# Output copies ahead of products, value products behind L1, and a last tile in two column halves

## The chip, the cores and the metric

The kernel runs on one core of a Trainium2 chip. The metric is the device time of one execution in microseconds (us). The kernel before takes 312.5 us (median; 312.0 to 312.8 over the first four runs). One run differs from the next by some tenths of a microsecond, so the questions of this case, which are about 0.1 to 1.2 us, are answered mostly from traces, stage by stage, and only in the sum from times.

Engines are called PE (matmul), DVE (vector), ACT (scalar, activation functions), POOL and SP (which here only starts transfers). PSUM is the memory that matmuls write to; this kernel keeps eight buffers of 512 float32 per partition in it, called banks below.

## The reference

```python
q_bucket, k_bucket = hash bits of q @ proj, k @ proj      # 6 bits each
scores = where(q_bucket == k_bucket, q @ k.T / 8, -1e9)   # 4 batches, 8 heads, 768 tokens, 64 wide
x = softmax(scores) @ v                                   # heads side by side: 3072 x 512
h = x @ w_in                                              # 512 -> 2048   ("L1")
g = h * cos(h)
out = g @ w_out                                           # 2048 -> 512   ("L2")
```

(abridged: the softmax and the reshape are written out in the original.) The output is 3072 x 512 in float32.

## The kernel before

All instructions are emitted in one fixed order, and each engine works through its own in that order. Attention runs head by head in 192 steps: a step makes scores on PE, exponentials on ACT, and value products on PE. L1 of a batch stands in one block inside the attention of the next. L2 of a batch is cut into single matmuls and filled into the gaps by `fill(n)`.

```python
def l1_ff(b, ff, hp):                 # one of 16 L1 tiles of a batch
    ...                               # 8 matmuls of 384 columns into the bank(s) hp
    for c_, g_, h_ in pieces:
        nc.scalar.activation(out=c_, in_=h_, func=ACTF.Sin, bias=cos_bias, scale=1.0)
    for c_, g_, h_ in pieces:
        nc.vector.tensor_tensor(out=g_, in0=h_, in1=c_, op=ALU.mult)   # the product
...
def l2_mm():                          # one L2 matmul; 16 make an output tile
    b, qt, ff = l2q.pop(0)
    if ff == 0 and not state["hold"]:
        state["m"] = 1 - state["m"]   # the other bank, except inside an L1 block
    ...
    if ff == NFF - 1:
        if b == B - 1 and qt == T - 1:            # last tile of all: two half copies
            nc.vector.tensor_copy(out=ob[:, 0:hw], in_=o_ps[:, 0:hw])
            nc.sync.dma_start(out=dst[:, 0:hw], in_=ob[:, 0:hw])
            nc.vector.tensor_copy(out=ob[:, hw:], in_=o_ps[:, hw:])
            nc.scalar.dma_start(out=dst[:, hw:], in_=ob[:, hw:])
        else:
            nc.vector.tensor_copy(out=ob, in_=o_ps)   # the output copy
            nc.sync.dma_start(out=dst, in_=ob)
...
state["hold"] = bb > 0                # the L1 block of batch bb
for ff in range(NFF):
    ...                               # choose the bank hp
    l1_ff(bb, ff, hp)
    ...
    if ff in (0, 1) and len(pend) > 0:
        av_step()                     # six value matmuls
    if bb > 0:
        fill(L1F(ff))                 # 3, 3, 2, 2, then 0, 1, 0, 1 ...
state["hold"] = False
l2_add(bb)
fill(ENDF)
```

The softmax here doesn't subtract the row's maximum and nothing guards it: scores larger than these inputs give would overflow.

Of the kernel before, what the change touches and what calls it, by code (L numbers as in the profile page):

```python
# [9 lines left out]
FP32 = mybir.dt.float32  # L10
# [3 lines left out]
ALU = mybir.AluOpType  # L14
# [8 lines left out]
def kernel(  # L23
# [10 lines left out]
    nc = tc.nc  # L34
    B, H, S, D = q.shape
    assert (B, H, S, D) == (4, 8, 768, 64)
    NBITS = proj.shape[1]
    D_MODEL = H * D
    D_FF = moe_w_out.shape[0]
    P = 128  # L40
    T = S // P
    NP = B * H // 2
    NFT = D_MODEL // P
    NFF = D_FF // P
# [6 lines left out]
    L1F = lambda ff: (3,3,2,2)[ff] if ff<4 else ff%2  # L51
    UF = lambda u: 2 if u % 2==0 else 1
    NEARLY = 5

    glob = ctx.enter_context(tc.tile_pool(name="glob", bufs=1))
    natp = ctx.enter_context(tc.tile_pool(name="nat", bufs=3))
# [10 lines left out]
    obp = ctx.enter_context(tc.tile_pool(name="ob", bufs=3))  # L67
# [3 lines left out]
    wout_t = [glob.tile([P, D_MODEL], FP16, name=f"wout{i}") for i in range(NFF)]  # L71
# [17 lines left out]
    s_ps = [psp.tile([P, 2, 512], FP32, name=f"s_ps{i}") for i in range(2)]  # L89
    av_ps = [psp.tile([P, 512], FP32, name=f"av_ps{i}") for i in range(2)]  # L90
    m_ps = [psp.tile([P, 512], FP32, name=f"m_ps{i}") for i in range(2)]
    state = {"m": 0, "rot": 0, "hold": False}

    nat, blk, bits = {}, {}, {}
    xn, xT = {}, {}
# [5 lines left out]
    def load(pr, eng):  # L101
        nat[pr] = []
        for src, nm in ((q, "natq"), (k, "natk"), (v, "natv")):
            t_ = natp.tile([P, 2, T * D], FP32, name=nm)
            eng.dma_start(out=t_, in_=heads_ap(src, pr))
            nat[pr].append(t_)
# [7 lines left out]
    def n16_rows(pr):  # L114
        return n16x_bufs[pr % 2].rearrange("p h w t e -> p (h w t e)")[:, 0:2 * T * 2 * D].rearrange(
            "p (h t w d) -> p h t w d", h=2, t=T, w=2)

    def cast_qk(pr, hh, engs):
        for w in range(2):
            if pr >= NEARLY:  # L120
                o_ = n16_rows(pr).rearrange("p h t w d -> p (h t) w d")[:, :, w, :]
# [10 lines left out]
    def cast_v(pr):  # L132
        vx = vx_bufs[pr % 3]
        nv = nat[pr][2].rearrange("p h (t d) -> p h t d", d=D)
        nc.gpsimd.tensor_copy(out=vx[:, :, :, 0:D], in_=nv)  # L135
        half = vsp.tile([P, 2, 3, D], FP32, name="vhalf")
        nc.gpsimd.tensor_tensor(out=half, in0=nv[:, :, 0:3, :], in1=nv[:, :, 3:6, :], op=ALU.add)  # L137
        two = vsp.tile([P, 2, D], FP32, name="vtwo")
        nc.gpsimd.tensor_tensor(out=two, in0=half[:, :, 0, :], in1=half[:, :, 1, :], op=ALU.add)
        nc.gpsimd.tensor_tensor(  # L140
            out=vs_bufs[pr % 3][:, :, 0:D], in0=two, in1=half[:, :, 2, :], op=ALU.add)
# [102 lines left out]
    def score(h, jt):  # L244
        pr, hh = divmod(h, 2)
        sp = s_ps[state["rot"] % 2]
        state["rot"] += 1
        for c, (c0, c1) in enumerate(((0, 512), (512, 768))):
            nc.tensor.matmul(  # L249
                out=sp[:, c, 0:c1 - c0],  # L250
                lhsT=kx(pr)[:, hh, jt * P:(jt + 1) * P],
                rhs=qx(pr)[:, hh, c0:c1],
                start=True, stop=True)
        pt = ptp.tile([P, S], FP16, name="pt")
        nc.scalar.activation(  # L255
            out=pt, in_=sp.rearrange("p c n -> p (c n)")[:, 0:S], func=ACTF.Exp,
            bias=exp_bias, scale=EXP_SCALE)
        pts[(h, jt)] = pt
# [52 lines left out]
    g_tiles = {}  # L311

    def l1_ff(b, ff, hp):
        halves = hp if isinstance(hp, list) else [hp[:, c, :] for c in range(2)]
        for ft in range(NFT):
            for c in range(2):
                nc.tensor.matmul(  # L317
                    out=halves[c][:, 0:C2],
                    lhsT=win_t[ft][:, ff * P:(ff + 1) * P],
                    rhs=xT[(b, ft)][:, 3 * c:3 * c + 3, :],  # L320
                    start=(ft == 0), stop=(ft == NFT - 1))
        cos = cosp.tile([P, 2, C2], FP16, name="cos")
        g = gp.tile([P, 2, C2], FP16, name="g")
        if isinstance(hp, list):
            pieces = [(cos[:, c], g[:, c], halves[c][:, 0:C2]) for c in range(2)]
        else:
            pieces = [(cos, g, hp[:, :, 0:C2])]
        for c_, g_, h_ in pieces:
            nc.scalar.activation(out=c_, in_=h_, func=ACTF.Sin, bias=cos_bias, scale=1.0)  # L329
        for c_, g_, h_ in pieces:  # L330
            nc.vector.tensor_tensor(out=g_, in0=h_, in1=c_, op=ALU.mult)  # L331
        g_tiles[(b, ff)] = g

    l2q = []

    def l2_add(b):
        l2q.extend((b, qt, ff) for qt in range(T) for ff in range(NFF))

    def l2_mm():
        b, qt, ff = l2q.pop(0)  # L340
        if ff == 0 and not state["hold"]:
            state["m"] = 1 - state["m"]
        o_ps = m_ps[state["m"]]
        g = g_tiles[(b, ff)].rearrange("p c n -> p (c n)")
        nc.tensor.matmul(  # L345
            out=o_ps, lhsT=g[:, qt * P:(qt + 1) * P], rhs=wout_t[ff],
            start=(ff == 0), stop=(ff == NFF - 1))
        if ff == NFF - 1:
            ob = obp.tile([P, D_MODEL], FP32, name="ob")
            dst = out.rearrange("(b p t) n -> b t p n", b=B, t=T)[b, qt]  # L350
            if b == B - 1 and qt == T - 1:
                hw = D_MODEL // 2
                nc.vector.tensor_copy(out=ob[:, 0:hw], in_=o_ps[:, 0:hw])
                nc.sync.dma_start(out=dst[:, 0:hw], in_=ob[:, 0:hw])
                nc.vector.tensor_copy(out=ob[:, hw:], in_=o_ps[:, hw:])
                nc.scalar.dma_start(out=dst[:, hw:], in_=ob[:, hw:])
            else:
                nc.vector.tensor_copy(out=ob, in_=o_ps)  # L358
                nc.sync.dma_start(out=dst, in_=ob)

    def fill(n):
        for i in range(n):
            if l2q and not (state["hold"] and i > 0 and l2q[0][2] == 0):
                l2_mm()

    def weights_in(i):
# [2 lines left out]
    def weights_out(i):  # L369
        nc.gpsimd.dma_start(out=wout_t[i], in_=moe_w_out[i * P:(i + 1) * P, :])  # L370

    pend = []
# [15 lines left out]
    with tc.manual_schedule():  # L388
# [29 lines left out]
        for b_ in range(4):  # L418
            nc.vector.tensor_copy(
                out=projblk[32 * b_:32 * b_ + 32, :, b_, 0:NBITS], in_=proj2)  # L420
# [30 lines left out]
        def at(u, f):  # L451
            acts.setdefault(u, []).append(f)
# [5 lines left out]
        for n in range(1, NP):  # L458
            s0 = 12 * (n - 1) - (0 if n < NEARLY else 4 if n == NEARLY else 6)
            def start(n=n):  # L460
                cast_qk(n, None, (nc.gpsimd, nc.gpsimd))
                blocks(n)
                cast_v(n)
            if n < NEARLY:
                at(s0 + 2, lambda n=n: load(n + 2, nc.sync if n + 2 < NEARLY else nc.gpsimd))
            elif NEARLY + 1 < n < NP - 1:
                at(s0 - 1, lambda n=n: load(n + 1, nc.gpsimd))
            if n < NEARLY:
                o_ = 3 if n == 1 else 0
# [34 lines left out]
        for u in range(U):  # L504
            h, jt = divmod(u, T)
            score(h, jt)
            pend.append((h, jt))
            for _ in range(2):
                if len(pend) > (4 if u < T else 2):
                    av_step()  # L510
            for f in acts.get(u, ()):
                f()
            b = u // UB
            if b > 0:
                fill(UF(u))
            if u in L1_AT:
                bb = L1_AT[u]
                state["hold"] = bb > 0
                for ff in range(NFF):
                    if bb == 0 and ff % 3 == 2:  # L520
                        hp = m_ps
                    elif ff % 3 == 2:
                        hp = [m_ps[1 - state["m"]], av_ps[0]]
                    else:
                        hp = s_ps[state["rot"] % 2]
                        state["rot"] += 1
                    l1_ff(bb, ff, hp)
                    if bb == 0:
                        nc.gpsimd.tensor_copy(out=mark, in_=g_tiles[(0, ff)][:, 0, 0:1])
                        if ff < NFF // 2:  # L530
                            weights_out(2 * ff)
                            weights_out(2 * ff + 1)
                        elif ff == NFF // 2:
                            load(NEARLY + 2, nc.gpsimd)
                    if ff in (0, 1) and len(pend) > 0:
                        av_step()
                    if bb > 0:
                        fill(L1F(ff))
                state["hold"] = False
                l2_add(bb)  # L540
                fill(ENDF)
# [4 lines left out]
        fill(1000)  # L546
        for ff in range(NFF):
            hp = (s_ps[0], m_ps, s_ps[1])[ff % 3]
            l1_ff(B - 1, ff, hp)
        l2_add(B - 1)  # L550
        fill(1000)

# [29 lines left out]
```

## Time and profile before

| before | value | how to read it |
|---|---|---|
| time | 312.5 us | the profiled run spans 310.8; the rest lies outside the span |
| PE busy | 97% of the span | matmul ends are modelled, so this is no measure of waits |
| PE waits on an output copy | 1.8 us, 2 times | the two at the starts of L1 of batches 1 and 2 |
| PE wait on a product | 0.3 us, once | the end of L1 of batch 0 |

**A ruler.** The trace shows a table load of 1.28 us on ACT each time that it changes between exponential and cosine. These loads stand at the borders of the stages, and their starts cut the run into pieces. Four of them in the timeline of ACT of the kernel before (start us, us, engine, line, operation):

```profile
126.19 1.28 ACT L329 ACT_TABLE_LOAD   x1
151.93 1.28 ACT L255 ACT_TABLE_LOAD   x1
196.50 1.28 ACT L329 ACT_TABLE_LOAD   x1
221.94 1.28 ACT L255 ACT_TABLE_LOAD   x1
```

L1 of batch 1 lasts from 126.19 to 151.93, 25.74 us; the attention after it 44.57; L1 of batch 2 25.44. The piece from the last table load (257.98) to the end of the span is called the last piece below: 310.8 - 257.98 = 52.82 us. Span ends are given to 0.1 us in the views, so a last piece is good to 0.05. Where that is too coarse, "by the records" below means times taken from the single instructions and landings in the packed trace, which are good to 0.01.

### The profile page before, as it was taken

The page shows a single profiled execution, that of the slowest core. Times are in us where ns is not written, and L with a number is a line of the kernel's source. Part 1 is how long each engine was busy: PE and PEld are TensorE (multiplying, and loading weights), DVE is VectorE, ACT ScalarE, POOL GpSimd, SP SyncE. Part 2 cuts the span into 40 slices and gives each one's busy share as a digit, 9 for nine tenths or more (in the row PEclk, how much of TensorE's full clock was granted, in tenths as well). Part 3 has the DMA queues.
Part 4 walks back from the last instruction along what each step waited for, and adds up shares of the span by engine and source line. Part 5 has one row for each costly group of instructions (what it writes and reads, how often), then busy time and mean ns, then how long its engine had stood idle before and what let it go on. Part 6 is the DMA issues. An engine that isn't in the chain of part 4 may idle for free.

```text
span 310.8 us, 7680 instructions
## 1 busy us (share of the span) xinstructions
PE 300.5 (97%) x3074; PEld 181.2 (58%) x3074; DVE 201.5 (65%) x434; ACT 234.1 (75%) x288; POOL 109.1 (35%) x180
## 2 busy tenths in 40 slices
PE   8899999899999999899999999999999999999995
PEld 3577667566566666555566666555566664565442
DVE  3665467877698988756677869757677343477211
ACT  3788999977899999666899999756899993477000
POOL 3897268288484584300064584100030000000000
PEclk9999999999999999999999999999999999999999
DMA  7959959399559976600168988100133222100121
GB/s 213 373 105 187 327 55 216 44 142 179 190 154 253 209 192 152 203 2 0 38 83 235 229 152 194 30 34 0 38 75 90 68 61 86 43 0 0 58 79 69
DMA packets 45332, 37.74 MB, mean 121 GB/s; under 512 B 32264, under 2 KB 39200, under 8 KB 45296
## 3 DMA queue, kind: packets, MB, share of 16 engines
q1 hardware_dynamic: 38080, 19.35, 28.5%
q0 software_dynamic: 6576, 17.17, 21.0%
q10 hardware_dynamic: 640, 0.72, 0.8%
q8 instruction: 24, 0.39, 0.5%
q14 instruction: 12, 0.10, 0.1%
HBM read 27.26 MB, written 6.29 MB: 108 GB/s over the span
## 4 chain that ended last, share of the span: by engine, by line
PE 84%; ACT 9%; DVE 3%; issue 2%; DVEq 0%; ACTq 0%
PE m_ps L345 25%; PE s_ps L317 17%; PE s_ps L249 17%; PE av_ps L275 9%; ACT pt L255 8%; PE m_ps L317 6%; PE m_ps L161 4%; PE av_ps L317 2%; PE s_ps L384 1%; PE m_ps L221 1%; ACT cos L329 1%; DVE ob L358 1%; DVE g L331 1%; DVE blkq L148 1%; PE av_ps L161 1%
## 5 line engine op out<-in xcount | busy, mean ns | idle before, releaser
L255 ACT ACTIVATE pt<-s_ps,exp_bias 128x768 f16<-128x768 f32 x192 | 161.6, 899 | 11.1 <-PE s_ps L249 9.7
L345 PE MATMUL m_ps<-wout,g 128*128 128x512 f16 x384 | 109.1, 379 | 2.1 <-DVE ob L358 1.8
L249 PE MATMUL s_ps<-qx,kx 128*128 128x512 f16 (+1 forms) x384 | 93.8, 326 | 2.6 <-ACT pt L255 1.2
L275 PEld LDWEIGHTS <-pt 128*128 128x128 f16 x1152 | 58.7, 97 | 21.7
L317 PEld LDWEIGHTS <-win 128*128 128x128 f16 x512 | 49.9, 98 | 34.4 <-issue 0.2
L275 PE MATMUL av_ps<-vx,pt 128*128 128x65 f16 x1152 | 65.7, 193 | 0.0
L317 PE MATMUL s_ps<-xT,win 128*128 128x384 f16 x352 | 62.3, 326 | 0.1
L331 DVE TENSOR_TENSOR g<-s_ps,cos 128x768 f16<-128x768 f32 x44 | 42.1, 957 | 29.9 <-ACT cos L329 29.9
L329 ACT ACTIVATE cos<-s_ps,cos_bias 128x768 f16<-128x768 f32 x44 | 39.6, 901 | 27.7 <-PE s_ps L317 26.4
L249 PEld LDWEIGHTS <-kx 128*128 128x128 f16 x384 | 35.2, 97 | 31.1 <-issue 3.3
L345 PEld LDWEIGHTS <-g 128*128 128x128 f16 x384 | 32.8, 98 | 24.4 <-issue 5.7
L135 POOL CAST vx<-natv 128x768 f16<-128x768 f32 x16 | 13.2, 827 | 95.2 <-PE av_ps L275 90.2
L358 DVE COPY ob<-m_ps 128x512 f32<-128x512 f32 x23 | 15.8, 685 | 22.0 <-PE m_ps L345 21.9
L317 PE MATMUL m_ps<-xT,win 128*128 128x384 f16 x120 | 27.6, 326 | 0.0
L329 ACT ACTIVATE cos<-m_ps,cos_bias 128x384 f16<-128x384 f32 x30 | 16.3, 578 | 8.4 <-PE m_ps L317 8.4
L302 DVE TENSOR_TENSOR xn<-tot,rc 128x384 f16<-128x384 f32 x24 | 20.1, 838 | 0.8
L331 DVE TENSOR_TENSOR g<-m_ps,cos 128x384 f16<-128x384 f32 x30 | 15.7, 550 | 2.1 <-ACT cos L329 1.8
L297 DVE COPY dv<-av_ps 128x65 f32<-128x65 f32 x24 | 5.1, 211 | 16.9 <-PE av_ps L275 16.9
L137 POOL TENSOR_TENSOR vhalf<-natv 128x384 f32<-128x384 f32 x16 | 15.9, 995 | 0.0
L130 POOL CAST n16x<-natk 128x768 f16<-128x768 f32 (+1 forms) x16 | 13.0, 810 | 5.8 <-DMA natk<-in_k_dram 5.8
L148 DVE STREAM_TRANSPOSE blkq<-natq 128x768 f32<-128x768 f32 x15 | 14.6, 975 | 0.3
L130 POOL CAST n16x<-natq 128x768 f16<-128x768 f32 (+1 forms) x16 | 13.1, 820 | 4.8 <-DMA natq<-in_q_dram 4.8
(76 smaller groups left out, 267.6 us busy)
## 6 DMA issues: line engine op xcount, KB each, us to landing
out_dram<-ob SPq DMA_DIRECT2D x23, 256.0 KB
natq<-in_q_dram POOLq DMA_DIRECT2D x11, 384.0 KB, 4.1
natk<-in_k_dram POOLq DMA_DIRECT2D x11, 384.0 KB, 4.7
natv<-in_v_dram POOLq DMA_DIRECT2D x11, 384.0 KB, 5.7
win<-in_moe_w_in_dram POOLq DMA_DIRECT2D x4, 512.0 KB, 7.3
wout<-in_moe_w_out_dram POOLq DMA_DIRECT2D x16, 128.0 KB, 4.8
natq<-in_q_dram SPq DMA_DIRECT2D x4, 384.0 KB
natk<-in_k_dram SPq DMA_DIRECT2D x4, 384.0 KB
```

Source lines behind the costliest of these rows:

```text
L130: engs[w].tensor_copy(out=o_, in_=i_)
L137: nc.gpsimd.tensor_tensor(out=half, in0=nv[:, :, 0:3, :], in1=nv[:, :, 3:6, :], op=ALU.add)
L148: nc.vector.transpose(out=blk[pr][w].rearrange("p h t c r -> p (h t c r)"), in_=nat[pr][w].rearrange("p h f -> p (h f)"))
L249: nc.tensor.matmul(out=sp[:, c, 0:c1 - c0], lhsT=kx(pr)[:, hh, jt * P:(jt + 1) * P], rhs=qx(pr)[:, hh, c0:c1], start=True, stop=True)
L255: nc.scalar.activation(out=pt, in_=sp.rearrange("p c n -> p (c n)")[:, 0:S], func=ACTF.Exp, bias=exp_bias, scale=EXP_SCALE)
L275: nc.tensor.matmul(out=bank[:, qt * W:qt * W + D + 1], lhsT=pt[:, qt * P:(qt + 1) * P], rhs=vx_bufs[pr % 3][:, hh, jt, 0:D + 1], start=Fal ...
L302: nc.vector.tensor_tensor(out=dst, in0=tot[:, :, 0:D], in1=rc.unsqueeze(2).to_broadcast([P, T, D]), op=ALU.mult)
L317: nc.tensor.matmul(out=halves[c][:, 0:C2], lhsT=win_t[ft][:, ff * P:(ff + 1) * P], rhs=xT[(b, ft)][:, 3 * c:3 * c + 3, :], start=(ft == 0) ...
L329: nc.scalar.activation(out=c_, in_=h_, func=ACTF.Sin, bias=cos_bias, scale=1.0)
L331: nc.vector.tensor_tensor(out=g_, in0=h_, in1=c_, op=ALU.mult)
L345: nc.tensor.matmul(out=o_ps, lhsT=g[:, qt * P:(qt + 1) * P], rhs=wout_t[ff], start=(ff == 0), stop=(ff == NFF - 1))
L358: nc.vector.tensor_copy(out=ob, in_=o_ps)
```

## The change

Three independent things are reordered. The products of the first two L1 tiles of batches 1 and 2 are emitted after the L2 matmuls that follow them, so that an output copy among those comes first on DVE. The second group of six value matmuls in the L1 block of batch 0 moves from tile 1 to behind tile 15. The last output tile is made as two tiles of 256 columns in the two banks, so that the first half is copied and sent while the second is computed.

```diff
+    AVS = ((0, 15), (0, 1))
+    GDEF = range(2)
@@ l1_ff
-        for c_, g_, h_ in pieces:
-            nc.vector.tensor_tensor(out=g_, in0=h_, in1=c_, op=ALU.mult)
+        def products():
+            for c_, g_, h_ in pieces:
+                nc.vector.tensor_tensor(out=g_, in0=h_, in1=c_, op=ALU.mult)
+        return products
@@ the last tile
+    def last_tile():
+        ...
+        for c, eng in ((0, nc.sync), (1, nc.scalar)):
+            cols = slice(c * hw, c * hw + hw)
+            o_ps = m_ps[c if state["m"] else 1 - c]
+            for ff in range(NFF):
+                ...
+                nc.tensor.matmul(out=o_ps[:, 0:hw], lhsT=g[:, S - P:S], rhs=wout_t[ff][:, cols], ...)
+            nc.vector.tensor_copy(out=ob[:, cols], in_=o_ps[:, 0:hw])
+            eng.dma_start(out=dst[:, cols], in_=ob[:, cols])
@@ the L1 block
-                    l1_ff(bb, ff, hp)
+                    products = l1_ff(bb, ff, hp)
...
-                    if ff in (0, 1) and len(pend) > 0:
+                    if ff in AVS[bb > 0] and len(pend) > 0:
                         av_step()
-                    if bb > 0:
+                    if bb > 0 and ff in GDEF:
+                        fill(L1F(ff))
+                        products()
+                    elif bb > 0:
+                        products()
                         fill(L1F(ff))
```

(cut: `l2_mm` calls `last_tile` for the last output tile, and its two half copies are gone; for batch 0 the products are called at once, as before; `fill` gained a switch, `COOL`, that is off.)

More of the change, by code (lines that the diff above doesn't have):

```diff
@@ L53 @@
     NEARLY = 5
+    AVS = ((0, 15), (0, 1))
+    GDEF = range(2)
+    COOL = False
     glob = ctx.enter_context(tc.tile_pool(name="glob", bufs=1))
@@ L91 @@
     m_ps = [psp.tile([P, 512], FP32, name=f"m_ps{i}") for i in range(2)]
-    state = {"m": 0, "rot": 0, "hold": False}
+    state = {"m": 0, "rot": 0, "hold": False, "cool": False}
     nat, blk, bits = {}, {}, {}
@@ L337, in l2_add @@
         l2q.extend((b, qt, ff) for qt in range(T) for ff in range(NFF))
+    def last_tile():
+        hw = D_MODEL // 2
+        ob = obp.tile([P, D_MODEL], FP32, name="ob")
+        dst = out.rearrange("(b p t) n -> b t p n", b=B, t=T)[B - 1, T - 1]
+        for c, eng in ((0, nc.sync), (1, nc.scalar)):
+            cols = slice(c * hw, c * hw + hw)
+            o_ps = m_ps[c if state["m"] else 1 - c]
+            for ff in range(NFF):
+                g = g_tiles[(B - 1, ff)].rearrange("p c n -> p (c n)")
+                nc.tensor.matmul(
+                    out=o_ps[:, 0:hw], lhsT=g[:, S - P:S], rhs=wout_t[ff][:, cols],
+                    start=(ff == 0), stop=(ff == NFF - 1))
+            nc.vector.tensor_copy(out=ob[:, cols], in_=o_ps[:, 0:hw])
+            eng.dma_start(out=dst[:, cols], in_=ob[:, cols])
     def l2_mm():
         b, qt, ff = l2q.pop(0)
+        if b == B - 1 and qt == T - 1:
+            if ff == 0:
+                last_tile()
+            return
         if ff == 0 and not state["hold"]:
@@ L350, in l2_mm @@
             dst = out.rearrange("(b p t) n -> b t p n", b=B, t=T)[b, qt]
-            if b == B - 1 and qt == T - 1:
-                hw = D_MODEL // 2
-                nc.vector.tensor_copy(out=ob[:, 0:hw], in_=o_ps[:, 0:hw])
-                nc.sync.dma_start(out=dst[:, 0:hw], in_=ob[:, 0:hw])
-                nc.vector.tensor_copy(out=ob[:, hw:], in_=o_ps[:, hw:])
-                nc.scalar.dma_start(out=dst[:, hw:], in_=ob[:, hw:])
-            else:
-                nc.vector.tensor_copy(out=ob, in_=o_ps)
-                nc.sync.dma_start(out=dst, in_=ob)
+            nc.vector.tensor_copy(out=ob, in_=o_ps)
+            nc.sync.dma_start(out=dst, in_=ob)
     def fill(n):
         for i in range(n):
-            if l2q and not (state["hold"] and i > 0 and l2q[0][2] == 0):
+            if COOL and l2q and state["hold"] and l2q[0][2] == 0 and not state["cool"]:
+                state["cool"] = True
+                return
+            if not COOL and l2q and state["hold"] and i > 0 and l2q[0][2] == 0:
+                return
+            if l2q:
+                state["cool"] = False
                 l2_mm()
@@ L534 @@
                             load(NEARLY + 2, nc.gpsimd)
-                    if ff in (0, 1) and len(pend) > 0:
+                    if ff in AVS[bb > 0] and len(pend) > 0:
                         av_step()
-                    if bb > 0:
+                    if bb > 0 and ff in GDEF:
+                        fill(L1F(ff))
+                        products()
+                    elif bb > 0:
+                        products()
                         fill(L1F(ff))
@@ L548 @@
             hp = (s_ps[0], m_ps, s_ps[1])[ff % 3]
-            l1_ff(B - 1, ff, hp)
+            l1_ff(B - 1, ff, hp)()
         l2_add(B - 1)
```

## The prediction

> **What bounds the kernel now.** I read the page from the busy shares to the chain of waits, then who waited for whom, then the timeline at the four places that the diff touches.
>
> The busy line and the first line of the chain of work that ended last:
>
> ```profile
> PE 300.5 (97%) x3074; PEld 181.2 (58%) x3074; DVE 201.5 (65%) x434; ACT 234.1 (75%) x288; POOL 109.1 (35%) x180
> PE 84%; ACT 9%; DVE 3%; issue 2%; DVEq 0%; ACTq 0%
> ```
>
> The tensor engine (PE) is the bound: 84% of the chain that sets the end. The vector engine (DVE) holds 3% of it, some 9 us, and only that, plus PE's few idle microseconds, is to be had by reordering. No matmul of size is taken away, so a gain near 2% (6.2 us) is already unlikely.
>
> Who made PE wait (total us, times, longest us), of the lines that the diff touches:
>
> ```profile
> PE m_ps L345 <- DVE ob L358: 1.8, 2, 1.0
> PE m_ps L345 <- DVE g L331: 0.3, 1, 0.3
> ```
>
> L345 is the L2 matmul, L358 the copy of a finished output tile out of PSUM (ob), L331 the product h*cos(h). So just three PE waits belong here: two on an output copy, one on a product. The timeline (start us, us, engine, line) around the first, at the start of L1 of batch 1:
>
> ```profile
> 126.92 0.59 PE L345 MATMUL m_ps<-wout,g 128*128 128x512 f16 x2
> 128.42 0.96 DVE L331 TENSOR_TENSOR g<-s_ps,cos 128x768 f16<-128x768 f32 x1 [0.83 <-ACT cos L329]
> 128.65 0.34 PE L275 MATMUL av_ps<-vx,pt 128*128 128x65 f16 x6
> 129.29 0.68 DVE L358 COPY ob<-m_ps 128x512 f32<-128x512 f32 x1
> 129.89 0.95 DVE L331 TENSOR_TENSOR g<-s_ps,cos 128x768 f16<-128x768 f32 x1
> 130.03 0.81 PE L345 MATMUL m_ps<-wout,g 128*128 128x512 f16 x3 [1.04 <-DVE ob L358]
> ```
>
> The reader is to see: the last two matmuls of an output tile are done at 127.51 (126.92 + 0.59), so its copy could run; but the product stands before it in DVE's order, waits 0.83 us for its cosine, and then runs 0.9 us. The next tile must use the same bank, so PE waits until 130.03. The second place, L1 of batch 2, where the tile ends one L1 tile later:
>
> ```profile
> 199.35 0.60 PE L345 MATMUL m_ps<-wout,g 128*128 128x512 f16 x2
> 200.38 0.96 DVE L331 TENSOR_TENSOR g<-s_ps,cos 128x768 f16<-128x768 f32 x1 [0.62 <-ACT cos L329]
> 200.92 0.33 PE L317 MATMUL av_ps<-xT,win 128*128 128x384 f16 x1
> 201.25 0.68 DVE L358 COPY ob<-m_ps 128x512 f32<-128x512 f32 x1
> 201.99 0.59 PE L345 MATMUL m_ps<-wout,g 128*128 128x512 f16 x2 [0.74 <-DVE ob L358]
> ```
>
> The third, L1 of batch 0: six value matmuls (L275) stand after its second tile, and at its end PE waits for the products of tile 14, which free the bank that L2 begins with:
>
> ```profile
> 61.92 0.34 PE L275 MATMUL av_ps<-vx,pt 128*128 128x65 f16 x6
> 62.10 1.46 PE L317 MATMUL m_ps<-xT,win 128*128 128x384 f16 x8
> 79.00 1.46 PE L317 MATMUL s_ps<-xT,win 128*128 128x384 f16 x8
> 79.71 1.01 DVE L331 TENSOR_TENSOR g<-m_ps,cos 128x384 f16<-128x384 f32 x2
> 80.78 1.46 PE L345 MATMUL m_ps<-wout,g 128*128 128x512 f16 x6 [0.31 <-DVE g L331]
> ```
>
> And the tail, after the last matmul (its modelled end is 307.02): two half copies one behind the other, then two output transfers; the span ends at 310.8.
>
> ```profile
> 307.05 0.42 DVE L353 COPY ob<-m_ps 128x256 f32<-128x256 f32 x1 [2.76 <-PE m_ps L345]
> 307.39 0.41 DVE L355 COPY ob<-m_ps 128x256 f32<-128x256 f32 x1
> 307.50 0.33 SPq L354 DMA_DIRECT2D out_dram<-ob  x1
> 307.84 0.36 ACTq L356 DMA_DIRECT2D out_dram<-ob  x1
> ```
>
> **What the Trainium skill says.** (1) "Perfetto Trace Analysis", section "Tensor Engine Instruction (MATMUL, LD_WEIGHTS)": a matmul's reported end is an estimate from its size. The idle figures in brackets (1.04, 0.74, 0.31) count from such ends, so I measure stalls from start to start instead. (2) "TensorE: Matmul & The Clock Gate", "Back-to-back issue gap": N/2.4 + 2.5 ns for N columns at full clock. The trace agrees: eight 384-column matmuls take 1.30 us on the chain, 162.5 ns each; 512 columns come every 216 ns; six 65-column ones take 0.18 us. (3) The same page, "Architectural detail": PE may pull weight loads ahead, ACT and DVE are strict FIFO. The trace agrees: the copy above was ready at 127.51 and sat behind a product until 129.29. (4) "DMA: Bandwidth & Descriptors", "Anatomy of one DMA": a fixed cost of about 2.0 us, most of it the wait until the last byte has landed. The trace has 2.6 us from the end of the last issue (307.84 + 0.36 = 308.20) to the span's end; nothing in the diff shortens that.
>
> **The change part by part.** On DVE exactly two instructions change places in the built programs: the copy moves ahead of the product of tile 0 in batch 1, and ahead of the product of tile 1 in batch 2. PE sees six value matmuls moved and the last tile split. ACT, POOL and SP keep their order.
>
> *Copy ahead of product, batch 1.* The value matmuls start at 128.65, six take 0.18 us, so PE was free at 128.83 and went on at 130.03: a stall of 1.20 us. Afterwards the copy starts when DVE has done the xn multiply before it (ends 127.59) and takes 0.69: done 128.28, 0.55 before PE asks. The product still starts at 128.42, its cosine comes no sooner. The whole 1.20 us goes.
>
> *Copy ahead of product, batch 2.* The last matmul of L1 tile 2 starts at 200.92, PE is free at 201.08 and went on at 201.99: 0.91 us. Afterwards the copy can start when the tile ends, about 200.0, and is done near 200.7, 0.4 before it is asked for. The product of tile 1 then starts near 200.7 instead of 200.38, so it ends some 0.3 later, near 201.65. Its bank is wanted by tile 4 only, some 1.5 us later; hidden. The whole 0.91 goes.
>
> *Value matmuls of batch 0.* L1 there is paced by PE: 14 tiles from 62.10 to 80.30 (79.00 + 1.30), 1.30 us each, just the matmuls. Taking out six value matmuls moves all of it 0.18 us earlier, the products of tile 14 with it. PE then reaches the end at 80.12, does the six until 80.30, and waits for the products until 80.60 instead of 80.78. The stall of 0.48 us (80.30 to 80.78) now holds 0.18 of work. Gain 0.18 us.
>
> *Last tile in two halves.* 16 matmuls of 512 columns (16 x 216 ns = 3.45 us) become 32 of 256 (32 x 109.2 ns, an estimate by point 2, = 3.49): 0.04 us more. The first half's copy and transfer go beside the second half's matmuls, so of the 0.34 us between the two copies' starts all leaves the end. Gain 0.34 - 0.04 = 0.30 us. The two banks are free: the copy of the tile before runs 303.60 to 304.29 and its bank is wanted about 305.2.
>
> Sum: 1.20 + 0.91 + 0.18 + 0.30 = 2.59 us, all on the path. Between these places attention is filled by the exponentials (48 of 0.9 us in the 43.4 us between the table loads of batches 0 and 1) and by PE nearly as full; both start from the end of L1, so an earlier end of L1 shifts both. 312.45 - 2.59 = 309.86.
>
> **Rivals.** *A new wait behind each removed one.* If PE came to L2 and found another product or a cosine missing, part of 1.20 and 0.91 would come back. For it: in batch 2 the product of tile 1 is late by 0.3. Against it: the margins above are 0.4 us or more, and ACT idles 0.83 to 2.3 us between cosines there. It would leave 310.3 to 311. *ACT or transfers as the bound of the attention stages.* If those stages had a clock of their own (loads of q, k, v; transposes by DMA), the 2.1 us won in L1 would be waited away later. For it: the chain goes through the exponentials for the last 9 us before L1 of batch 1. Against it: the exponentials start only after the cosines of that L1, so they shift too; PE waited 0.2 us for a transfer in the whole run after the start. It would make 311.5. *A tail that gains more.* The two last transfers were issued 0.34 us apart and shared the engines; afterwards the last has them alone. Up to 0.3 us more, 309.5. *The value matmuls where they stood filled a wait.* Then moving them gains nothing: 310.0. Against it, the 62.10 start follows them with no gap.
>
> **Range and chances.** I take 309.9. Three runs before spread over 0.58 us, so the median alone is good to some 0.3; loss of one small part or a better tail moves it by 0.3 more; one rival of the first kind costs 0.4 to 0.7. Range 309.3 to 310.6. A gain of 2% is 6.2 us, more than twice all the stalls concerned; a loss of 2% would need new stalls of 6 us where none has a source. Faster 0.01, same 0.98, slower 0.01.
>
> **What would show it.** Right: no PE wait on ob in either L1 of batches 1 and 2; the copy starting before the product; L1 of batches 1 and 2 shorter by 1.2 and 0.9 us; of batch 0 by 0.18, with the six value matmuls just ahead of the first L2 matmul; one copy of 256 columns after the last matmul, and the last issue 0.3 us sooner after it. Wrong: a PE wait on g, cos or a score bank of like size, attention stages longer than before, or 256-column matmuls spaced wider than 109 ns. A run in which weights load slower than they are used would show the last.

## The result, and the profile after

The changed kernel takes 310.1 us (median of 4; 309.95 to 310.51) against 312.51 (4 runs). The ratio is 0.9927, 95% interval 0.9909 to 0.9944. By the 2% rule that is "same"; it is a gain of 0.7%.

The ruler in the kernel after:

```profile
125.96 1.28 ACT L332 ACT_TABLE_LOAD   x1
150.51 1.28 ACT L258 ACT_TABLE_LOAD   x1
195.07 1.28 ACT L332 ACT_TABLE_LOAD   x1
219.62 1.28 ACT L258 ACT_TABLE_LOAD   x1
```

| piece | before, us | after, us | gain |
|---|---|---|---|
| start to L1 of batch 0 | 59.87 | 59.86 | 0.01 |
| L1 of batch 0 | 21.55 | 21.36 | 0.19 |
| attention | 44.77 | 44.74 | 0.03 |
| L1 of batch 1 | 25.74 | 24.55 | 1.19 |
| attention | 44.57 | 44.56 | 0.01 |
| L1 of batch 2 | 25.44 | 24.55 | 0.89 |
| attention | 36.04 | 36.04 | 0.00 |
| last piece | 52.82 | 52.74 | 0.08 |

The gains add to 2.40 us, the difference of the two spans (310.8 - 308.4). By the records the spans are 310.79 and 308.42 and the last pieces 52.81 and 52.75, so the gain in the last piece is 0.05 and the whole 2.37. No attention stage grew, so nothing is given back there. The view of who made PE wait has four lines left for the whole run, and none names an output copy or a product h*cos(h). The start of L1 of batch 1, in the timeline after:

```profile
126.69 0.59 PE L370 MATMUL m_ps<-wout,g 128*128 128x512 f16 x2
127.32 0.69 DVE L376 COPY ob<-m_ps 128x512 f32<-128x512 f32 x1
128.19 0.96 DVE L337 TENSOR_TENSOR g<-s_ps,cos 128x768 f16<-128x768 f32 x1 [0.18 <-ACT cos L332]
128.42 0.34 PE L278 MATMUL av_ps<-vx,pt 128*128 128x65 f16 x6
128.60 0.81 PE L370 MATMUL m_ps<-wout,g 128*128 128x512 f16 x3
```

The copy (L376) now runs at 127.32, as soon as its tile is done and DVE free, in the time in which the product had waited for its cosine. PE goes from the value matmuls to L2 at 128.60, with no bracket behind the line: no wait. Batch 2:

```profile
197.93 0.59 PE L370 MATMUL m_ps<-wout,g 128*128 128x512 f16 x2
198.56 0.69 DVE L376 COPY ob<-m_ps 128x512 f32<-128x512 f32 x1 [0.23 <-PE m_ps L370]
199.17 0.95 DVE L337 TENSOR_TENSOR g<-s_ps,cos 128x768 f16<-128x768 f32 x1
199.66 0.59 PE L370 MATMUL m_ps<-wout,g 128*128 128x512 f16 x2
```

The copy is done at 199.25, 0.4 us before L2 asks for the bank at 199.66. The end of L1 of batch 0:

```profile
79.51 1.01 DVE L337 TENSOR_TENSOR g<-m_ps,cos 128x384 f16<-128x384 f32 x2
80.10 0.34 PE L278 MATMUL av_ps<-vx,pt 128*128 128x65 f16 x6
80.58 1.46 PE L370 MATMUL m_ps<-wout,g 128*128 128x512 f16 x6
```

The six value matmuls now stand in the wait for the product, which ends at 80.52, and L2 starts 0.20 us sooner than the 80.78 of before. And the tail:

```profile
301.08 3.66 PE L354 MATMUL m_ps<-wout,g 128*128 128x256 f16 x32
303.02 0.42 DVE L357 COPY ob<-m_ps 128x256 f32<-128x256 f32 x1 [1.05 <-PE m_ps L354]
304.77 0.42 DVE L357 COPY ob<-m_ps 128x256 f32<-128x256 f32 x1 [1.32 <-PE m_ps L354]
305.23 0.36 ACTq L358 DMA_DIRECT2D out_dram<-ob  x1
```

One half copy follows the last matmul, as meant. The last output is issued 49.57 us into the last piece (305.23 - 255.66), before it was 49.86 (307.84 - 257.98): 0.29 us sooner. Yet the last piece is only 0.08 shorter. From the last issue to the end there are 3.17 us, before there were 2.96 (3.19 and 2.95 by the records). That is the one part of the sum that did not come, and most experiments are about it.

SP's own waits show what happens there: SP waits for the output transfers to land and then goes through a closing exchange with the other engines. Asked in steps of 0.05 us, they come in this order, in the kernel before (waiter, what it waited for, us in total, times, longest):

```profile
SPq L577 <- DMA out_dram<-ob: 1.1, 1, 1.1
SPq L577 <- PEq L577: 0.2, 1, 0.2
```

and in the kernel after:

```profile
SPq L606 <- DMA out_dram<-ob: 1.7, 1, 1.7
SPq L606 <- PEq L606: 0.2, 1, 0.2
```

In the kernel after, the 1.7 us wait ends near 307.0, which is 1.75 us after the last issue at 305.23, and the wait of 0.2 on PE's sequencer ends near 307.85. In the kernel before, the wait of 1.1 us is for the first half (issued 307.50, landed 309.25, 1.75 later); no wait is shown for the second, but the record of its landing stands at 309.59, again 1.75 after its issue, and the exchange follows at 310.15. So the last half landed as fast as before. But 0.85 us instead of 0.55 went by between landing and exchange. What fills them is shown at the end of the experiments.

### The profile page after: what moved, and what is told of

It is laid out like the page before. It is cut to its first block, busy times and chain, and to the rows that moved or that the text cites. A ratio compares the mean times of both kernels' runs of the same rounds, so it can differ in the third digit from the quotient of the medians.

```text
span 308.4 us, 7711 instructions
## 1 busy us (share of the span) xinstructions
PE 300.1 (97%) x3090; PEld 182.8 (59%) x3090; DVE 201.8 (65%) x434; ACT 234.3 (76%) x288; POOL 109.4 (35%) x180
## 4 chain that ended last, share of the span: by engine, by line
PE 89%; ACT 6%; DVE 3%; issue 1%; ACTq 0%; DVEq 0%
PE m_ps L370 26%; PE s_ps L320 18%; PE s_ps L252 18%; PE av_ps L278 10%; PE m_ps L320 6%; ACT pt L258 5%; PE m_ps L164 4%; PE av_ps L320 2%; PE s_ps L408 1%; PE m_ps L354 1%; PE m_ps L224 1%; DVE g L337 1%; DVE blkq L151 1%; ACT cos L332 1%; PE av_ps L164 1%
## 5 line engine op out<-in xcount | busy, mean ns | idle before, releaser
L370 PE MATMUL m_ps<-wout,g 128*128 128x512 f16 x368 | 105.6, 379 | 0.1
L370 PEld LDWEIGHTS <-g 128*128 128x128 f16 x368 | 31.2, 98 | 20.1 <-issue 3.3
L376 DVE COPY ob<-m_ps 128x512 f32<-128x512 f32 x23 | 15.8, 686 | 22.6 <-PE m_ps L370 22.6
```

What stands on the lines that cost most here:

```text
L370: nc.tensor.matmul(out=o_ps, lhsT=g[:, qt * P:(qt + 1) * P], rhs=wout_t[ff], start=(ff == 0), stop=(ff == NFF - 1))
```

## The experiments

Twelve runs were made (the changed kernel and the split issued by SP ran twice), all with correct results. The first four were timed in five rounds on one chip, the last two on another; the others had one look. The edits are against the changed kernel unless it is said otherwise.

**The changed kernel again.**

> The changed kernel once more, as the yardstick of this group. Theory A (the four gains of 1.20, 0.91, 0.18 and 0.30 us add): 2.59 us under the kernel before, ratio 0.9917. Theory B (the 0.30 us won ahead of the last issue are given back between that issue and the end, as the profile hints: 3.17 us there against 2.96 before): 2.29 us under, ratio 0.9927.

It took 310.15 us against 312.56, ratio 0.9925 (0.9891 to 0.9959). The pieces came out as in the first trace: 21.37, 24.55 and 24.54 for the three L1 blocks, 52.73 for the last piece; the issue at 49.57, the end 3.16 after it. The time spoke for theory B, but with an interval this wide it could not decide; the trace did.

**The last tile not split.**

```diff
-        if b == B - 1 and qt == T - 1:
-            if ff == 0: last_tile()
-            return
+            # the two half copies of the kernel before, at ff == NFF - 1
```

> The changed kernel with the last output tile as before (one bank, two copies one after the other). Theory A: 0.30 us slower than the changed kernel of this group. Theory B: equal to it. Either way 2.29 us under the kernel before, and 2.96 us from the last output issue to the end of the span.

It took 310.12 us, ratio 0.9923 (0.9892 to 0.9954): not to be told from the changed kernel. Its last piece is 52.79 us, with the issue at 49.86 and the end 2.93 after it. Its L1 blocks are those of the changed kernel. So the split is worth about 0.06 us here (0.02 by the records), close to B.

**The split alone.** (`GDEF = ()`, `AVS = ((0, 1), (0, 1))`.)

> The kernel before with the split last tile alone. Theory A: 0.30 us faster than before (ratio 0.9990). Theory B: no difference (1.0000), with the last issue 0.30 us nearer to the last matmul but the end of the span 0.2 to 0.3 us further from the last issue.

The ratio was 1.0004 (0.9964 to 1.0043). The L1 blocks are as in the kernel before (21.54, 25.74, 25.45). The last piece is 52.78 us, with the issue at 49.56 and the end 3.22 after it. The halves behave the same without the other changes: 0.30 us won before the issue, some 0.25 lost behind it.

**The two copies alone.** (`AVS` and the last tile as before.)

> The kernel before with the two output copies moved ahead of the products alone. Both theories: 1.20 + 0.91 = 2.11 us faster (ratio 0.9932), no wait of the tensor engine on ob left, and the wait of 0.3 us on the product at the end of L1 of batch 0 as before. A rival (the attention stages have a bound of their own that takes the gain back): less than 1 us.

The ratio was 0.9919 (0.9887 to 0.995), 310.17 us. L1 of batch 1 took 24.54 and of batch 2 24.55 us, L1 of batch 0 21.54, and the wait of 0.3 us on the product was there as before. The two moves of a copy are worth 1.20 and 0.89 us by the ruler (2.09 together, 2.11 expected), nearly the whole gain. The attention stages stayed at 44.70, 44.58 and 36.03 us, so the rival that they take the gain back falls. Against this kernel, the one without the split differs only in the value matmuls, and its L1 of batch 0 is 21.37: they are worth 0.17.

**PE busy for longer.** Six traces now fitted a formula: the end comes at the later of the last matmul's end + 3.66 and the last issue + 2.95. Three kernels tested it.

```diff
         fill(1000)
+        warmup(4)          # four matmuls of zeros into a free bank
```

> The changed kernel with four idle matmuls of 512 columns into a free bank after the last output matmul (4 x 216 ns = 0.86 us of tensor engine, nothing waits for them). Model M (the span ends at the later of two chains: end of the last matmul + 3.66 us, and issue of the last output + 2.95 us; it fits the six traces so far to 0.1): from the last table load to the end 52.74 + 0.86 = 53.60 us, from the last output issue to the end 4.03. Model F (the split's last transfer simply takes 3.17 us because it runs alone): no change, 52.74 and 3.17.

The last piece was 53.09 us, neither 53.60 nor 52.74; the end came 3.52 us after the issue. SP's wait for the output transfers now ended 2.4 us after the last issue instead of 1.75. By the records 15 of the 16 parts of the last transfer had landed by 1.82; the sixteenth still moved data until 1.99 (before: 1.40) and landed at 2.40. So it was a late landing that moved the end, by 0.35 where M wants 0.86; F, with no change, fails too. An 8 KB packet of the kind "instruction" ran from 1.07 to 1.64, beside this transfer; in the other traces it overlaps the last transfer by 0.05 us at most. That it held up the sixteenth part, and that PE's later end had a share in it, is not shown.

**The last issue later.**

```diff
-            nc.vector.tensor_copy(out=ob[:, cols], in_=o_ps[:, 0:hw])
+            for _ in range(1 + c):
+                nc.vector.tensor_copy(out=ob[:, cols], in_=o_ps[:, 0:hw])
```

> The changed kernel with the last half copy done twice, which puts the last output issue 0.34 us later and leaves the tensor engine alone. Model M: the issue chain overtakes by 0.13, so 52.87 us from the last table load to the end and 2.95 from the last issue. Model F: 53.08 and 3.17.

The second copy cost 0.46 us, not 0.34: the two to one place did not overlap, as the two to different places had done in the kernel before. With the issue 0.46 later the end came 0.25 later: 52.99 us, 2.96 after the issue. F with 0.46 would be 53.20, M 52.98. That looks like 0.2 us of slack in the last issue, and it is not: the transfer landed 1.80 us after its issue, 0.07 more than in the changed kernel, and the end followed the landing by 1.15 us instead of 1.46. The records at the end of this section say why.

**An uneven cut, 384 + 128 columns.**

> The changed kernel with the last tile cut 384 + 128 columns instead of 256 + 256. The last copy takes about 0.28 in place of 0.42 us (an estimate from 0.69 for 512 and 0.42 for 256 columns), so the last issue comes 0.14 sooner. Model M: no gain, 52.74 us from the last table load, 3.3 from the last issue. Model F: 52.60 and 3.17 or less.

The issue came 0.14 us sooner, as meant, and the last piece was 52.53, 0.2 shorter. With the tensor engine's end where it was (49.07 us into the piece, 49.08 in the changed kernel), M allows no gain. M falls: it was a fit. The 3.10 us from issue to end contain a smaller last transfer, which landed about 1.6 us after its issue; the 0.85 between landing and exchange are there as in the changed kernel.

**A score ahead of the L2 matmuls after L1 of batch 0.** This was meant as an improvement.

```diff
             score(h, jt)
+            if late: fill(late.pop())
...
-                fill(ENDF)
+                late.append(ENDF) if bb == 0 else fill(ENDF)
```

> The changed kernel with the six L2 matmuls after L1 of batch 0 put behind the next score, so that the score (0.33 us) fills the 0.3 us that the tensor engine still waits there for a product. If the tensor engine paces the attention of batch 1, it is 0.3 us shorter (44.4 in place of 44.7 us from table load to table load); if the exponentials pace it, no change.

It missed. PE had no wait left at that place (the score ran at 80.33, L2 at 80.66), but the attention stage took 44.88 us, 0.18 longer than the 44.70 expected without a gain and 0.14 longer than in the first trace of the changed kernel. The view of PE's waits has a new one of 0.3 us, a score waiting for the transfer of hash bits. A wait taken from PE at this place buys nothing; of the two causes offered, the trace shows the new wait and doesn't exclude the exponentials.

**The issuers of the halves exchanged.**

```diff
-        for c, eng in ((0, nc.sync), (1, nc.scalar)):
+        for c, eng in ((0, nc.scalar), (1, nc.sync)):
```

> The changed kernel with the issuers of the two halves exchanged: the first half from ACT, the last from SP. The last output has so far landed 1.75 us after its issue in the split and in the unsplit kernel, but the end followed the landing by 1.4 us in the split and by 1.2 in the unsplit one. Theory S (what follows the landing depends on SP, which sits in the closing waits early in the split; issuing the last transfer itself, it comes there as late as in the unsplit kernel): 2.95 us from the last issue to the end, 52.5 us from the last table load. Theory R (it is the closing of the program after the tensor engine's end, whoever issues): 3.17 and 52.74.

The last piece was 52.71 us, with 3.15 from issue to end. That is R's number: S falls, since SP came to its closing waits last and it didn't help. (R does not last: see the next run.)

**Both halves issued by SP.** (`nc.sync` twice.)

> The changed kernel with both halves issued by SP and none by ACT. Theory S: 2.95 us from the last issue to the end, 52.5 from the last table load. Theory R: 3.17 and 52.74. If instead the second issue of the same engine waits for the first transfer, the last issue comes later than 49.57 us after the last table load.

The issue came at 49.56, so the second issue did not wait for the first transfer, and the last piece was 52.36 us, with 2.80 from issue to end. The exchange follows the landing by 0.5 us instead of 0.85. This is against R, and also shorter than S had it.

**The same, timed, and the fourth corner.** In the second of these kernels the last tile is unsplit, and `nc.scalar` in its second transfer becomes `nc.sync`.

> The split with both halves issued by SP once more, timed, as the version meant to beat both kernels. If the one look was no accident: 52.36 us from the last table load to the end again, 2.8 from the last issue, and 2.2 + 0.4 = 2.7 us under the kernel before (ratio about 0.9915, against 0.9925 of the changed kernel, which these rounds can hardly tell apart). If it was: 52.74 and 3.17.

> The changed kernel with the last tile unsplit and both its half transfers issued by SP: the fourth corner beside split and unsplit with two issuers and split with one. If one issuer shortens the closing by itself: 49.86 + 2.80 = 52.66 us from the last table load to the end, so split with one issuer gains its full 0.30. If the closing was long only in the split with two issuers: 49.86 + 2.95 = 52.81, as unsplit with two.

The first repeated the look: 52.35 us. It took 309.89 us, ratio 0.9917 (0.9902 to 0.9932), the best of all measured, and by the interval faster than the kernel before by 0.7 to 1.0%. The rounds do not set it apart from the changed kernel (0.9925 to 0.9927); the last piece does, in two traces. Its timeline and SP's two last waits but one:

```profile
303.26 2.08 SPq L358 DMA_DIRECT2D out_dram<-ob  x2
304.56 0.42 DVE L357 COPY ob<-m_ps 128x256 f32<-128x256 f32 x1 [1.32 <-PE m_ps L354]
SPq L606 <- DMA out_dram<-ob: 0.7, 1, 0.7
SPq L606 <- PEq L606: 0.2, 1, 0.2
```

The first line merges two issues; the second starts at 303.26 + 2.08 - 0.33 = 305.01. The 0.7 us wait for the landing ends near 306.75, and the wait on PE's sequencer is there by 307.2.

The second had a last piece of 52.84 us (issue at 49.94, end 2.90 after it), so one issuer does not shorten an unsplit tail. Its profiled run, the slowest of its six (313.06), began 2 us late (61.79 us to the first L1) and had an attention stage of 45.60 with a wait of 0.7 us on hash bits; its ratio (0.9942, median 310.59) includes that run and is not used. The four corners of the last piece:

| last tile | ACT issues one half | SP issues both |
|---|---|---|
| unsplit | 52.79 to 52.84 us (three kernels) | 52.84 |
| split | 52.71 to 52.78 (five traces, either order of issuers) | 52.35, 52.36 |

The split is worth 0.48 us with one issuer (0.45 by the records) and under 0.1 with two. (The uneven cut is left out of the table.)

**What the records of SP show.** No run was made for this question, but the 14 traces settle what the exchange waits for. SP itself is late. Between its 207th and its 208th instruction it pauses for 0.36 to 0.38 us, and the 208th starts later than the last semaphore that it waits for: by 0.05 to 0.08 us in three traces, by the whole pause in nine. (In the other two the 208th waits longer than that for the last landing.) The pause belongs to the place in SP's list and not to what stands there: the split with one issuer has two more SP instructions ahead, and there the pause comes two waits earlier. What counts is whether SP pauses before or after it has seen the last landing.

| SP's instructions in all | kernels | the pause | last landing to end, us |
|---|---|---|---|
| 215 | changed (twice), split alone, score first, issuers exchanged, uneven | after the wait for the last landing, in full | 1.46 to 1.49 |
| 216 | before, unsplit, copies alone | just before that wait; it ends 0.05 to 0.08 after the landing | 1.18 to 1.19 |
| 216 | PE busy for longer, last issue later | the same place, inside the wait for the landing | 1.15 |
| 217 | split issued by SP (twice) | two waits earlier than in the first row, over before the landing | 1.12, 1.13 |
| 218 | unsplit issued by SP | three waits earlier, over before the landing | 1.12 |

The changed kernel has one closing instruction of SP fewer than the kernel before, so the pause fell behind the last landing, and 0.27 of the 0.32 us by which the last half landed sooner went into it. SP as the only issuer moved it ahead of that landing again.

## Why the prediction was right, and which term was off

- **The bound and the size of what is to be had.** Right. The engine named, the three waits and the order of magnitude hold. 309.9 was said, 310.1 measured, inside the range.
- **Copy ahead of product, batch 1 (1.20) and batch 2 (0.91).** Right: 1.19 and 0.89 by the ruler, 1.20 and 0.89 with that part alone. Counting stalls from start to start was what made this exact: the brackets, 1.04 and 0.74, are smaller by the modelled ends of the matmuls.
- **Value matmuls (0.18).** Right: 0.19 in the first trace, 0.17 between two kernels that differ in nothing else.
- **Last tile in halves (0.30).** The step that failed is "so of the 0.34 us between the two copies' starts all leaves the end". The copy left the path: the issue came 0.29 sooner and the transfer landed 1.73 us after it (1.75 before). But the end followed the issue by 3.17 us instead of 2.96, so 0.08 reached the end (0.05 by the records). The term was mis-sized by 0.22 to 0.25 us, and with it the sum: 2.59 against 2.40 between the two spans. The prediction took the 2.6 us after the last issue as one piece that the diff leaves alone. They are two, a landing and a closing exchange, and the diff changed the second: it put SP's pause of 0.36 us behind the last landing.
- **Rivals.** A new wait behind each removed one did not appear. The attention stages kept their length, so nothing was taken back there. "A tail that gains more" had the wrong sign: the tail gained less, and the last transfer, alone in the engines, landed 1.73 us after its issue against 1.75. That the value matmuls stood in a wait already falls with the 0.17.
- **Small misreadings.** The prediction has ACT idle at least 0.83 us between the cosines; in its own first place the trace has 0.46 (before the cosine at 128.85). Between the end of the first table load and the start of the next there are 43.5 us, not 43.4. Nothing hangs on either.
- **What stays open.** Why SP pauses at that place. SP pauses in the same way between its 79th and 80th instruction (0.44 to 0.45 us in all 14 traces), 128 instructions earlier, and 1.0 to 1.3 us after it enters the later pause an 8 KB packet of the kind "instruction" starts, in every trace (after the earlier pause the next one comes 2.2 to 3.8 us later). "Runtime: NRT & Kernel Launch", "Instruction fetch mechanics", says that an engine's sequencer fetches the next block of its instructions by a DMA queue of its own while it executes, and that crossing a block's border costs one bump of the queue's tail, mostly hidden. The page has blocks of 16 KiB or 256 instructions; the 8 KB and the 128 of this trace are half of that. That the pause is such a border fits, but no run moved it on purpose, so it is not shown.

## What to carry to other kernels

On an engine that works in order, an instruction that waits for a late input blocks what stands behind it; if that is a copy which frees a PSUM bank, the matmul engine pays. Look for a copy whose input is done long before it starts, and emit it ahead of the waiting instruction. At the end of a program, moving the last issue is not moving the end: measure issue, landing and closing apart, and look where the engine that closes the program stands when the last transfer lands. Here one issuing engine was worth nearly 0.4 us with the split tail and nothing with the unsplit one: only in the split tail did it move a pause of SP ahead of that landing.

## What the Trainium skill lacked or had wrong

- "TensorE: Matmul & The Clock Gate", "Back-to-back issue gap", gives about 131 ns per matmul of 512 columns for a stream of weight loads and matmuls. Here such a stream runs at 216 ns, and the formula that the page keeps for isolated matmuls fits: 109.3 ns at 256 columns (32 in 3.66 us less the modelled 0.27 of the last, over 31), 162.5 at 384.
- "DMA: Bandwidth & Descriptors", "Anatomy of one DMA", puts the fixed part at about 2.0 us, worked out on transfers that GpSimd issues. The outputs here are issued by SP and ACT: 128 KB landed 1.69 to 1.80 us after the start of the issue in 12 traces (2.40 in the one with PE busy for longer), with data moving for about 0.5 us of it. For these the section has no figure.
- No page tells of the program's own closing, which passes here inside the span: 1.12 to 1.49 us from the last landing to the end. None gives a time for a pause like SP's, 0.36 to 0.38 us at its 208th instruction and 0.44 to 0.45 at its 80th.
